# An FFT stage ahead of two MLPs: finer input transfers, six stores issued by ScalarE, two weight decodings begun a step later

## The chip, the cores and the metric

The kernel runs on one core of one Trainium2 chip. The metric is the device time of one execution in microseconds (us), as the median of several runs. An execution is the whole program: inputs from HBM, all compute, output back to HBM.

## The reference

`x` is (2, 3008, 256), float32. Three stages follow each other: a convolution along the sequence by FFT with a given filter, a gated MLP, and a second MLP. The MLP weights arrive as 64-bit floats.

```python
X = np.fft.rfft(x, axis=1)
y = np.fft.irfft(X * (filt_r + 1j * filt_i)[None], n=3008, axis=1)   # 2 x 3008 tokens of 256
g = t @ w_gate; t = (g / (1 + exp(-g)) * (t @ w_val)) @ w_out        # 256 -> 1536 -> 256
h = t @ w_in;   t = (h * clip(h + 3, 0, 6) / 6) @ w_out2             # 256 -> 2048 -> 256
```

## The kernel before

The change lies wholly in the first 80 us, in which the FFT stage runs as matrix products; the MLPs, over 90% of the time, follow. The order of every engine's work is written out by hand: each engine executes its own list in program order, and SyncE (SP) does nothing but issue DMA transfers.

**The FFT stage.** The 256 columns of each of the 2 batches are cut in 8, which gives 16 inputs. A loop `for k in range(N + 2)` with N = 16 does at step k: `over_n1(k)`, 64 small TensorE products of input k (L337), whose result ScalarE copies out of PSUM into a tile `y` (L348, L349); `back(k - 2)`, 16 products (L384), whose result ScalarE copies into `turned` (batch 0) or `turned_b` (batch 1) (L389); then the DMA issues listed for this step; `over_n2(k)`, 16 products that read ScalarE's copies (L357); and `filter_product(k)`, four VectorE products (L370) with sums on GpSimd. `back(k - 2)` needs the `filter_product` of two steps earlier. Inputs 0 to 7 alternate between the batches; 8 to 11 are batch 0's upper columns, 12 to 15 batch 1's.

**What sets the order of the transfers.** `send(k, ...)` enters a DMA issue in the list of step k. `load_x(k + 3)` (L296) fetches an input three steps ahead into `ring`, which holds four inputs; `pieces` says in how many transfers. `load_filter` (L300) fetches the filters. `load_dec` (L407) fetches a weight block in three parts. `store(b, a, i)` (L393) writes an eighth of one half of `turned` to a DRAM tile `d2`: batch 0's lower half (a = 0) at steps 9 to 12, its upper half (a = 1) at step 13. `load_lower` (L465) at step 13 reads batch 0's lower half back in another layout, in four transfers, once the lower stores have landed; at step 15 `load_half` (L465) reads the upper half back, once the upper stores have landed. `form` (L158) turns what was read into the tokens of the first MLP block.

Transfers are given one of eight completion counters, DMAHW0 to DMAHW7, in turn. A transfer is issued only after the transfer that had the same counter before it has landed; so at most eight are under way, over SP and ScalarE together.

**The decoding of weights.** A 64-bit weight block is turned into float32 by `Decode`: `start` is one ScalarE pass over the loaded words (L189), six VectorE parts follow (L198 to L208 and L119). `todo` holds the steps of the first three blocks: the tuple's first number is the step of `start`, the next ones those of the parts.

After step 17 the first MLP begins (L234 first layer, L242 second); the later MLP loop is at L705 and L750.

```python
pieces = 4 if 4 <= k < 9 else 2                        # L290, of load_x
send(13, store, 0, 1, i)                               # L448, i = 0 to 7
```

Of the kernel before, what the change touches and what calls it, by code (L numbers as in the profile page):

```python
# [16 lines left out]
P = 128  # L17
# [60 lines left out]
def fft_conv_glu_mlp(ctx: ExitStack, tc: tile.TileContext, x, filt, mats, sgn, w1, w2, out):  # L78
    nc = tc.nc
# [23 lines left out]
    d2 = [dram.tile([NK, P, D], F32, name=f"d2_{b}") for b in range(B)]  # L103
# [164 lines left out]
    with tc.manual_schedule():  # L268
# [9 lines left out]
        turned = work.tile([P, 7168], F32, tag="xs", name="turned")[:, :6144].rearrange("p (a q c) -> p a q c", a=2, c=P)  # L278
        turned = [turned, top.tile([P, 6144], F32, tag="top", name="turned_b").rearrange("p (a q c) -> p a q c", a=2, c=P)]
# [6 lines left out]
        def load_x(k, engines=(nc.sync, nc.sync)):  # L286
            b, j = STEPS[k]
            if k % 2 == 0:
                xin[k // 2] = ring[:, k // 2 % RING * 2048:(k // 2 % RING + 1) * 2048].rearrange("p (a n) -> p a n", a=2)
            pieces = 4 if 4 <= k < 9 else 2  # L290
            to, src = (v.rearrange("p (o i n) -> p i o n", o=2, i=2) if k < 2 else v.rearrange("p (i n) -> p i n", i=pieces)
                       for v in (xin[k // 2][:, k % 2], x[b, j // 2, :, j % 2]))
            for i in range(pieces):
                if (k, i) == (1, 1):
                    nc.sync.dma_start(out=mat[:, CO:], in_=mats[:, CO:])
                engines[i % 2].dma_start(out=to[:, i], in_=src[:, i])  # L296

        def load_filter(j):
            for r in range(2):
                nc.sync.dma_start(out=fl[j // 4][:, j % 4, r], in_=filt[j][:, r])  # L300

        load_x(0, (nc.scalar, nc.sync))
        load_x(1, (nc.scalar, nc.sync))
        nc.sync.dma_start(out=sg, in_=sgn)
        load_filter(0)
        load_x(2)
        load_filter(1)
        load_x(3)
# [79 lines left out]
            for r in range(2):  # L388
                nc.scalar.copy(out=to[:, r], in_=accs[r][:, :2 * COLS].rearrange("p (o c q) -> p q o c", o=2, q=NK))  # L389

        def store(b, a, i):
            q = slice(i * NK // 8, (i + 1) * NK // 8)
            nc.sync.dma_start(out=d2[b][q, :, a * P:(a + 1) * P].rearrange("q p c -> p q c"), in_=turned[b][:, a, q])  # L393

        def words(a):
            return a.bitcast(U32).rearrange("p (n t) -> p n t", t=2)
# [28 lines left out]
        def at(k, step, *a):  # L425
            todo.setdefault(k, []).append(lambda: step(*a))

        def send(k, *a):
            moves.setdefault(k, []).append(a)
# [15 lines left out]
        send(13, load_lower)  # L445
        for i in range(8):
            send((9, 10, 10, 10, 11, 11, 11, 12)[i], store, 0, 0, i)
            send(13, store, 0, 1, i)  # L448

        for f, steps in ((0, (4, 5, 6, 6, 7, 8, 9, 10, 10)), (1, (10, 11, 11, 12, 12, 13, 14, 15, 17)), (2, (15, 15, 15, 17))):  # L450
            at(steps[0], lambda f: dec[f].start(), f)
            for i in range(len(steps[1:7])):
                at(steps[1 + i], lambda f, i: dec[f].part(i, nc.vector), f, i)
            if f < 2:
                at(steps[7], high_w1, f)
                at(steps[8], low_w1, f)
            else:
                for i in range(3, 6):
                    at(N + 1, lambda f, i: dec[f].part(i, nc.vector), f, i)
# [52 lines left out]
        steps = [(s % 2, s // 2) for s in range(2 * G1)]  # L512
# [76 lines left out]
        for t in range(2 * plain):  # L589
            p, i = divmod(t, 2)  # L590
            k, g_ = steps[p]
            f = 2 * g_ + i
# [67 lines left out]
            if 0 < t < 9:  # L660
                for i in range(2):
                    store(1, (t - 1) // 4, (t - 1) % 4 * 2 + i)
# [4 lines left out]
            if 10 < t < 23:  # L667
                q, r = divmod(t - 11, 2)
# [86 lines left out]
        class Plain:  # L755
            kind, k, f, n, last = 0, 0, 0, 512, True
# [105 lines left out]
        pieces = [(g, i) for g in range(G2) for i in range(2)]  # L862
# [19 lines left out]
        for s in range(S):  # L882
# [15 lines left out]
            k, f, n, kind = u.k, u.f, u.n, u.kind  # L898
# [127 lines left out]
```

## Time and profile before

| | us |
|---|---|
| median of 3 runs (1118.36 to 1119.36) | 1118.71 |
| the profiled execution | 1119.17 |
| its span, first to last instruction | 1117.2 |
| TensorE (PE) busy in the span | 1108.1 (99%) |
| VectorE (DVE), ScalarE (ACT), GpSimd (POOL) busy | 862.4, 750.2, 597.7 |

Times inside the trace count from the start of the span. "SPq" and "ACTq" are an engine's issuing of DMA; such an issue is not counted as busy, but the engine does nothing else meanwhile. "Landing" is the time from the issue to the completion of a transfer. The granted TensorE clock is 1.00 throughout, the upper one of its two levels (1.2 and 2.4 GHz).

### The profile page before, as it was taken

How to read it: one execution, taken by the hardware profiler on the slowest of the kernel's cores; microseconds unless marked ns; L12 is line 12 of the kernel's file. 1: busy time of each engine (PE TensorE's matmuls, PEld its weight loads, DVE VectorE, ACT ScalarE, POOL GpSimd, SP SyncE). 2: the span in 40 equal slices, each digit the busy share in tenths (PEclk: the TensorE clock that was granted, in tenths of full speed). 3: DMA queues.
4: the chain of work that ended last, by engine and by line, in shares of the span. 5: the costliest groups of instructions: out<-in, count | busy, mean ns of one | idle time of the engine just before them, and what ended most of it. 6: DMA issues, size and time to landing. Idle time of an engine off the chain costs nothing.

```text
span 1117.2 us, 19201 instructions
## 1 busy us (share of the span) xinstructions
PE 1108.1 (99%) x7237; PEld 921.4 (82%) x7237; DVE 862.4 (77%) x1178; ACT 750.2 (67%) x1363; POOL 597.7 (53%) x773
## 2 busy tenths in 40 slices
PE   9999999999999999999999999999999999999998
PEld 6778888888888888888899888888888888888997
DVE  5989977888878888786888868667677677677765
ACT  4555447667667667766777777777776677677764
POOL 3742376795765576484587645335435444354440
PEclk9999999999999999999999999999999999999999
DMA  7977845843733552263353421422322312412300
GB/s 247 313 214 226 251 167 167 233 151 123 191 119 112 154 169 100 83 203 108 104 206 116 166 81 58 154 78 71 135 78 78 143 63 78 149 52 78 116 27 33
DMA packets 60428, 150.75 MB, mean 135 GB/s; under 512 B 5872, under 2 KB 28880, under 8 KB 58576
## 3 DMA queue, kind: packets, MB, share of 16 engines
q1 hardware_dynamic: 59648, 148.78, 41.7%
q8 instruction: 56, 0.92, 0.3%
q10 hardware_dynamic: 688, 0.75, 0.2%
q14 instruction: 36, 0.29, 0.1%
HBM read 117.27 MB, written 32.24 MB: 134 GB/s over the span
## 4 chain that ended last, share of the span: by engine, by line
PE 94%; DVE 3%; DMA 2%; issue 1%; ACT 0%; POOL 0%; SPq 0%; DVEq 0%; ACTq 0%; POOLq 0%
PE gv L705 44%; PE a L750 36%; PE gv L234 5%; PE a L242 3%; PE a L357 1%; PE gv L158 1%; PE gv L384 1%; PE gv L337 1%; DMA x<-w_in 1%; DVE h L732 1%; DVE hs L116 1%; DMA ring<-x_in 0%; DVE xs L116 0%; DVE h L370 0%; DVE raw L116 0%
## 5 line engine op out<-in xcount | busy, mean ns | idle before, releaser
L705 PE MATMUL gv<-xs,wu 128*128 128x512 f32 (+1 forms) x2268 | 567.1, 386 | 0.2 <-DVE gv L119 0.2
L116 POOL TENSOR_TENSOR wu<-st,wu 128x224 fp32r<-128x224 f32 x432 | 310.4, 750 | 397.5 <-ACT wu L538 397.5
L705 PEld LDWEIGHTS gv<-xs,wu 128*128 128x128 f32 x2268 | 423.5, 188 | 81.8 <-ACT raw L567 1.7
L750 PE MATMUL a<-hs,wo 128*128 128x512 f32 (+1 forms) x1872 | 476.9, 385 | 0.0
L750 PEld LDWEIGHTS a<-hs,wo 128*128 128x128 f32 x1872 | 351.2, 188 | 65.8 <-ACT hs L738 0.5
L116 DVE TENSOR_TENSOR hs<-h,hs 128x512 fp32r<-128x512 f32 (+3 forms) x228 | 235.1, 1031 | 66.3 <-ACT hs L738 62.5
L738 ACT CAST hs<-h 128x512 fp32r<-128x512 f32 (+3 forms) x216 | 172.5, 799 | 130.2 <-DVE h L734 73.9
L116 POOL TENSOR_TENSOR wo<-st,wo 128x256 fp32r<-128x256 f32 x156 | 150.9, 980 | 0.0
L734 DVE SCALAR_TENSOR_TENSOR h<-h,gv 128x512 f32<-128x512 f32 (+1 forms) x144 | 96.4, 670 | 23.0 <-ACT h L728 22.7
L538 ACT CAST wu<-st 128x384 fp32r<-128x384 f32 x216 | 110.6, 563 | 0.4 <-DMA st<-w1f 0.4
L726 ACT ACTIVATE h<-gv 128x512 f32<-128x512 f32 (+1 forms) x120 | 70.6, 588 | 56.4 <-PE gv L705 54.9
L119 DVE TENSOR_TENSOR gv<-gv,h 128x512 f32<-128x512 f32 (+1 forms) x108 | 74.0, 685 | 40.5 <-PE gv L705 34.2
L728 ACT ACTIVATE h<-gv 128x512 f32<-128x512 f32 (+1 forms) x144 | 84.0, 583 | 15.6 <-PE gv L705 15.4
L915 ACT COPY gv<-gv 128x512 f32<-128x512 f32 (+1 forms) x108 | 60.9, 564 | 42.6 <-PE gv L705 38.7
L119 DVE TENSOR_TENSOR h<-gv,h 128x512 f32<-128x512 f32 (+1 forms) x108 | 73.0, 676 | 18.3 <-PE gv L705 17.8
L734 DVE SCALAR_TENSOR_TENSOR h<-h,h 128x512 f32<-128x512 f32 (+1 forms) x48 | 32.7, 681 | 58.6 <-ACT h L728 58.6
L919 ACT COPY h<-gv 128x512 f32<-128x512 f32 (+1 forms) x108 | 62.5, 578 | 16.1 <-PE gv L705 13.0
L732 DVE TENSOR_TENSOR h<-h 128x512 f32<-128x512 f32 (+1 forms) x60 | 62.2, 1037 | 1.5 <-ACT h L726 1.0
L116 DVE TENSOR_TENSOR xs<-raw,xs 128x512 fp32r<-128x512 f32 (+1 forms) x77 | 58.2, 757 | 0.1
L538 ACT CAST wo<-st 128x256 fp32r<-128x256 f32 (+1 forms) x108 | 54.2, 501 | 0.0
L581 ACT CAST xs<-raw 128x512 fp32r<-128x512 f32 (+1 forms) x77 | 45.6, 608 | 2.9 <-DVE raw L116 2.8
L234 PE MATMUL gv<-xs,wall_a 128*128 128x512 f32 x192 | 46.0, 393 | 0.3 <-ACT xs L123 0.2
(97 smaller groups left out, 890.4 us busy)
## 6 DMA issues: line engine op xcount, KB each, us to landing
st<-w1f SPq DMA_DIRECT2D x60, 576.0 KB, 3.8
st<-w2f SPq DMA_DIRECT2D x48, 704.0 KB, 4.1
raw<-w_in SPq DMA_DIRECT2D x16, 512.0 KB, 4.6
x<-w_in SPq DMA_DIRECT2D x9, 768.0 KB, 5.3
ring<-x_in SPq DMA_DIRECT2D x20, 256.0 KB, 5.5
yd<-y SPq DMA_DIRECT2D x5, 1024.0 KB, 6.6
raw<-yd SPq DMA_DIRECT2D x5, 1024.0 KB, 6.1
y_out<-y SPq DMA_DIRECT2D x20, 256.0 KB, 2.0
```

The costliest lines, as they stand in the source:

```text
L116: (engine or nc.vector).tensor_tensor(out=out, in0=a, in1=b, op=ALU.subtract)
L119: (engine or nc.vector).tensor_tensor(out=out, in0=a, in1=b, op=ALU.add)
L234: nc.tensor.matmul(acc, w[:, r, c[k]:c[k] + P], xs[:, v, k], start=(r, v, k) == (0, 0, 0), stop=(r, k) == (1, 1), skip_group_check=len(dep ...
L538: nc.scalar.copy(out=to[:, 0, at:at + hi - lo], in_=src[:, lo:hi])
L705: nc.tensor.matmul(acc[:, :n], w[:, r, FORM[a] * P:(FORM[a] + 1) * P], xs_part(k, v, i), start=start and q == 0, stop=q == 2, skip_group_c ...
L726: nc.scalar.activation(out=self.value(t, 0), in_=src, func=AF.Silu)
L728: nc.scalar.activation(out=self.value(t, a), in_=src, func=AF.Relu, bias=3.0)
L732: nc.vector.tensor_tensor(out=self.value(t, 0), in0=self.value(t, 0), in1=src, op=ALU.mult)
L734: nc.vector.scalar_tensor_tensor(out=self.value(t, a), in0=self.value(t, a), scalar=6.0, in1=src, op0=ALU.min, op1=ALU.mult)
L738: nc.scalar.copy(out=self.hs[:, t, :, 0, :self.n], in_=self.value(t))
L750: yield lambda t=t, v=v, a=a, j=j, r=r: nc.tensor.matmul(banks["a"][2 * j + t][:, :n], self.wo[:, r, (2 * a + j) * P:(2 * a + j + 1) * P], ...
L919: nc.scalar.copy(out=u.s7, in_=b3[:, :n])
```

## The change

Three things are changed. Inputs 9 to 15 (the tenth to the sixteenth) come in four transfers of 128 KB, as inputs 4 to 8 do, and no longer in two of 256 KB. Of the eight upper stores of batch 0, the first two stay on SP at step 13, three are issued by ScalarE at step 13 and three by ScalarE at step 14. `start` of the first weight block moves from step 4 to step 5, that of the second from step 10 to step 11; their VectorE parts stay.

```diff
-            pieces = 4 if 4 <= k < 9 else 2
+            pieces = 2 if k < 4 else 4
...
-        def store(b, a, i):
+        def store(b, a, i, engine=nc.sync):
             q = slice(i * NK // 8, (i + 1) * NK // 8)
-            nc.sync.dma_start(out=d2[b][q, :, a * P:(a + 1) * P].rearrange("q p c -> p q c"), in_=turned[b][:, a, q])
+            engine.dma_start(out=d2[b][q, :, a * P:(a + 1) * P].rearrange("q p c -> p q c"), in_=turned[b][:, a, q])
...
         send(13, load_lower)
         for i in range(8):
             send((9, 10, 10, 10, 11, 11, 11, 12)[i], store, 0, 0, i)
-            send(13, store, 0, 1, i)
+            send(13 + i // 5, store, 0, 1, i, nc.sync if i < 2 else nc.scalar)
-        for f, steps in ((0, (4, 5, 6, 6, 7, 8, 9, 10, 10)), (1, (10, 11, 11, 12, 12, 13, 14, 15, 17)), (2, (15, 15, 15, 17))):
+        for f, steps in ((0, (5, 5, 6, 6, 7, 8, 9, 10, 10)), (1, (11, 11, 11, 12, 12, 13, 14, 15, 17)), (2, (15, 15, 15, 17))):
             at(steps[0], lambda f: dec[f].start(), f)
```

ScalarE before, from the copies of `back(11)` at step 13 to those of `back(12)` at step 14 (what stands in brackets is what the row waits for):

```order
L389 COPY turned<-gv_106 128x24x16 [waits PE_49]
L389 COPY turned<-gv_107 128x24x16 [waits PE_49]
L348 COPY y<-gv_108 128x8x48 [waits PE_49,Activation_49]
L349 ACTIVATE y<-gv_108 128x8x24 [waits Activation_49]
L348 COPY y<-gv_109 128x8x48 [waits PE_49,Activation_49]
L349 ACTIVATE y<-gv_109 128x8x24 [waits Activation_49]
L389 COPY turned_b<-gv_106 128x24x16 [waits PE_49]
L389 COPY turned_b<-gv_107 128x24x16 [waits PE_49]
```

Nothing stands between the copies of `back(11)` and those of input 14 (`gv_` are PSUM banks, `d_0` below is batch 0's `d2`). ScalarE after the change, the same stretch and the stores of step 14:

```order
L389 COPY turned<-gv_107 128x24x16 [waits PE_49]
L393 DMA d_0_78<-turned 128x3x128 [waits DMAHW1_49,Activation_49]
L393 DMA d_0_78<-turned 128x3x128 [waits DMAHW3_49]
L393 DMA d_0_78<-turned 128x3x128 [waits DMAHW5_49]
L348 COPY y<-gv_108 128x8x48 [waits PE_49]
L349 ACTIVATE y<-gv_108 128x8x24
L348 COPY y<-gv_109 128x8x48 [waits PE_49]
L349 ACTIVATE y<-gv_109 128x8x24
L389 COPY turned_b<-gv_106 128x24x16 [waits PE_49]
L389 COPY turned_b<-gv_107 128x24x16 [waits PE_49]
L393 DMA d_0_78<-turned 128x3x128 [waits DMAHW6_49]
L393 DMA d_0_78<-turned 128x3x128 [waits DMAHW7_49]
```

Three stores stand ahead of the copies of input 14 (L348), and each has a counter to wait for; a third one of step 14 waits for DMAHW0.

SP after the change, steps 12 and 13, from the weight loads on:

```order
L407 DMA x_121<-w_in 128x512 [waits DMAHW1_49]
L393 DMA d_0_78<-turned 128x3x128 [waits DMAHW2_49]
L413 DMA w1f_86<-x_121 128x768 [waits DMAHW3_49,DVE_49]
L407 DMA x_121<-w_in 128x512 [waits DMAHW4_49]
L465 DMA g<-d_0_78 48x6x128 [waits DMAHW5_49,DMAHW2_49]
L465 DMA g<-d_0_78 48x6x128 [waits DMAHW6_49]
L465 DMA y<-d_0_78 48x6x128 [waits DMAHW7_49]
L465 DMA y<-d_0_78 48x6x128 [waits DMAHW0_49]
L393 DMA d_0_78<-turned 128x3x128 [waits Activation_49]
L393 DMA d_0_78<-turned 128x3x128 [waits DMAHW4_49]
```

Each row but the last but one waits for, and then takes, the counter named first. So the counter that ScalarE's third store waits for, DMAHW5, is the one taken by the first transfer of `load_lower` (the first L465 row), and DMAHW6, DMAHW7 and DMAHW0 are those of its other three. That first L465 row also waits for DMAHW2, the last lower store (the L393 row above it). TensorE's, VectorE's and GpSimd's orders are the same as before.

## Rows read from the trace of the kernel before

**Rows 1.** Busy time by stretch: PE, PEld, DVE, ACT, POOL, PE clock, DMA share, GB/s.

```profile
16.00:24.00 8.00, 8.00 (x222) 6.47 (x218) 5.16 (x12) 4.22 (x12) 4.49 (x8) 1.00 0.82 251
...
32.00:40.00 8.00, 7.72 (x212) 5.84 (x205) 7.96 (x14) 4.29 (x12) 6.29 (x9) 1.00 1.01 334
...
88.00:96.00 8.00, 8.00 (x37) 6.63 (x36) 7.80 (x10) 3.72 (x7) 1.93 (x2) 1.00 0.84 247
```

**Rows 2.** Waits, first 82 us: who, for whom, us in total, times, longest.

```profile
ACT x L189 <- DMA x<-w_in: 2.3, 1, 2.3
```

**Rows 3.** Timeline of PE: start, us, work, idle time before it and its releaser.

```profile
23.48 1.47 PE L384 MATMUL gv<-h,mat 64*64 64x384 f32 x14
25.86 1.78 PE L357 MATMUL a<-y,mat 64*64 64x384 f32 x14 [0.91 <-ACT y L348]
...
28.72 1.47 PE L384 MATMUL gv<-h,mat 64*64 64x384 f32 x14
...
45.05 0.39 PE L337 MATMUL gv<-mat,ring 48*64 48x48 f32 x12 [1.18 <-issue]
...
61.80 1.75 PE L357 MATMUL a<-y,mat 64*64 64x384 f32 x16
...
65.44 1.75 PE L357 MATMUL a<-y,mat 64*64 64x384 f32 x16
...
74.16 0.89 PE L158 MATMUL a<-mat,g 48*64 48x47 f32 x46 [0.26 <-DMA g<-d]
```

**Rows 4.** Timeline of ScalarE at steps 13 and 14.

```profile
58.50 0.86 ACT L389 COPY turned<-gv 128x384 f32<-128x384 f32 x2
60.90 0.48 ACT L348 COPY y<-gv 128x384 f32<-128x384 f32 x1 [1.54 <-PE gv L337]
...
62.15 0.86 ACT L389 COPY turned_b<-gv 128x384 f32<-128x384 f32 x2
```

**Rows 5.** Timeline of SP's DMA issues: start, us, how many in a row.

```profile
7.70 3.49 SPq L296 DMA_DIRECT2D ring<-x_in  x6
...
25.40 1.80 SPq L296 DMA_DIRECT2D ring<-x_in  x4
...
28.25 0.85 SPq L296 DMA_DIRECT2D ring<-x_in  x2
...
51.02 0.39 SPq L393 DMA_DIRECT2D d<-turned  x1
...
57.94 1.02 SPq L465 DMA_DIRECT2D g<-d  x2
...
60.06 5.65 SPq L393 DMA_DIRECT2D d<-turned  x8
69.61 0.83 SPq L465 DMA_DIRECT2D g<-d  x2
```

**Rows 6.** Waits of SP's own queue in the first 84 us.

```profile
SPq L465 <- DMA d<-turned: 8.6, 3, 4.9
...
SPq L300 <- DMA ring<-x_in: 2.1, 4, 0.7
```

**Rows 7.** One issue at 30.23; fetches of PE's instructions in 30.0:31.3 and in 28:58.

```profile
30.23 1.43 SPq L296 DMA_DIRECT2D ring<-x_in  x1
...
q8 instruction: 1, 0.02, 5.9%
...
q8 instruction: 6, 0.10, 1.3%
```

**Rows 8.** Landing: medians by size; the store issued at 51.02; the read at 57.94.

```profile
d<-turned SPq DMA_DIRECT2D x16, 192.0 KB, 4.9
ring<-x_in SPq DMA_DIRECT2D x20, 128.0 KB, 4.3
...
DMA to landing us min/median/max: 6.9/6.9/6.9
...
DMA to landing us min/median/max: 2.7/2.7/2.7
```

## The prediction

> **What bounds the kernel now.** Read the stretches first [rows 1]. From 88 us on TensorE is busy 8.00 of 8.00 us, and the order of its work there is not touched: whatever the front stage gives or costs is passed on whole to the end, unless a wait further on absorbs it. So only the first 80 us count. There TensorE steps along with ScalarE, VectorE and GpSimd in steps of 65.44 − 61.80 = 3.64 us when nothing holds it [rows 3], and the DMA engines are full in the middle: share 1.01 in 32:40 [rows 1].
>
> Then the waits. TensorE's idle time that bears on the change is short: 0.91 us at 25.86 behind ScalarE [rows 3], where ScalarE stood 2.3 us in front of the first weight's `start` (L189) until its load had landed [rows 2]; 1.18 us at 45.05, with no engine that released it; 0.26 us at 74.16, for batch 0's upper half read back [rows 3]. ScalarE at steps 13 and 14 is idle 1.54 us between its copies at 58.50 (0.86 us) and those at 60.90 [rows 4]: that is all the room that the three stores have.
>
> Last, SP's queue. Its largest wait is that of the reads of `d2` (L465) for stores to land: 8.6 us in three, 4.9 at most; filter loads (L300), which need nothing of the ring, wait 2.1 us for ring loads, which is the rule of eight counters at work [rows 6]. The last lower store is issued at 51.02 [rows 5] and needs 6.9 us [rows 8], so it lands at 57.9; at once, at 57.94, `load_lower` goes out [rows 5], and its first transfer lands 2.7 us later [rows 8], at 60.7.
>
> **Part 1, the `start` steps: a gain of 1.6 us at step 6.** From `back(3)` at 23.48 to `back(4)` at 28.72 is 5.24 us in place of 3.64 [rows 3]. The 1.6 us more are ScalarE's wait for the load and what it pushes along. A step later the load is long there, so the wait goes; the second block's `start` moves behind copies into ScalarE's idle 1.5 us a step and costs nothing. The cover for that is this idle time; if it were gone, the cost would be at most the 1.54 us of it [rows 4] that the pass fills.
>
> **Part 2, four transfers for two: what SP and the DMA engines pay.** Seven inputs get two more issues each, 14 in all, and all of them stand ahead of the last lower store. From the issue at 28.25 (first transfer of input 9) to the one at 51.02 there are 33 issues now [rows 5]; there will be 47, so 46 intervals. The price of one interval is bounded thus: 0.475 us, the six issues from 25.40 to 28.25, none of which shows a hold; 0.66 us, the 31 issues from 7.70 to 28.25, nearly all the stretch in which inputs came in four transfers already [rows 5]. I take a value between, and build it from below: an issue that falls into a fetch of TensorE's instructions is held, 1.43 us for the one at 30.23, with one such fetch in 30.0:31.3, and six fetches lie in 28:58 [rows 7]. That is 46 × 0.475 + 6 × (1.43 − 0.43) = 27.9 us, 0.61 each, nearer to the upper end, which is the row of like work. The store is issued at 28.25 + 27.9 = 56.1. With landings as they are for stores, 4.9 us by the median [rows 8], it lands at **61.0**, 3.1 us later than now.
>
> Two ends for that. If SP's queue is no limit, the DMA engines are: 7 × 512 KB at the rate of the stretch with small pieces, 251 / 0.82 = 306 GB/s, not at that with large ones, 334 / 1.01 = 331 [rows 1], is 12.0 in place of 11.1 us, so 0.9 us more and a landing at 58.8. At 0.66 us an issue it is 28.25 + 30.4 + 4.9 = 63.5. The inputs themselves are hidden: the last piece of input 15 is the 44th issue, at about 54.5, and lands 4.3 us later [rows 8], at 58.8; its products come after those at 61.80 [rows 3], or at 60.2 if TensorE runs 1.6 us early. If that cover went, TensorE would wait in `over_n1` too, but behind the same SP queue, and the time lost would overlap with Part 3.
>
> **Part 3, the six stores on ScalarE: a new wait.** ScalarE's third store of step 13 waits for the counter that `load_lower`'s first transfer took, so for its landing; the copies of input 14 stand behind it, and `over_n2(14)`, and with it all of TensorE, behind these. No transfer of batch 0's upper half needs that; it is the turn of the counters alone. With the lower half stored at 61.0, the first transfer of `load_lower` lands at 61.0 + 2.75 = 63.75; the third store is issued, about 0.5 us (the eight at 60.06 took 5.65 with one of them held, [rows 5]); the copies start at 64.3 and not at 60.90 [rows 4]: **3.4 us later**, whatever TensorE had gained before. That is the point: the 1.6 us of Part 1 only lengthen the wait at step 14. VectorE and GpSimd are fed by the same products and shift along. At step 14 the three other counters have landed by then; three issues of 0.5 us after the copies at 62.15 + 3.4 (0.86 us, [rows 4]) end at about 67.9, which is when input 15's products end, so a few tenths at most.
>
> After that one thing is absorbed. The upper stores are out at 67.9 and land at about 72; the read back goes out some 2.5 us later than now (69.61, [rows 5]), while TensorE is 3.4 us later, so the 0.26 us at 74.16 go. Sum: 3.4 − 0.26 = +3.1 us on the profiled execution of 1119.17, that is 1122.3. That execution is 0.46 us above the median of 1118.71, so I give 1118.71 + 3.1 = **1121.8**. The ends of Part 2 give 58.8 + 3.3 − 60.9 − 0.26 = +0.9 (1119.6) and 63.5 + 3.3 − 60.9 − 0.26 = +5.6 (1124.3).
>
> **The rivals.** A measurement of this kernel tells about 0.2%, 2.24 us, from no change; slower means above 1120.95, faster below 1116.47.
>
> *DMA bytes alone set the landing (0.27).* Issues run ahead of the DMA engines as they do now, the lower half lands at 58.8 and the step-14 copies are 1.2 us late: 1119.6, within 0.2%. For it: the present 6.9 us of that store show a queue in front of the DMA engines. Against: with 128 KB pieces an issue carries little more work than it costs. A rule of the Trainium skill would lead here: "Runtime: NRT & Kernel Launch", section "Instruction fetch mechanics", has the sequencer fetch its next 16 KiB by itself, a crossing "mostly hidden". By it the six holds would not be there, the issue would be at 28.25 + 21.9 = 50.1 and this rival's 1119.6 the result. The 1.43 us issue beside a fetch speaks against it, so I keep the holds.
>
> *The wait costs nothing, and the gains stay: faster (0.07).* Part 1's 1.6 us, the 0.26 us, and with shorter queues part of the 1.18 us at 45.05, say 0.6: 1118.71 − 2.5 = 1116.2. It decides itself at `load_lower`'s first landing: before 58.8 (60.4 less 1.6) it hides in ScalarE's idle time, for which the lower half must have landed by 56.0, almost 2 us earlier than now with 14 more issues ahead of it. Nothing in the rows moves it that way.
>
> *The stop also costs TensorE its clock (0.15).* TensorE would stand still over 4 us at step 14 (ready by 60.2, released after 64.3). No stop after the start is longer than 1.2 us now and the granted clock is 1.00 in every row, so the trace shows no price; bounded by nothing lost, and by one step of 3.64 us run at the lower of the two levels, which takes twice as long: 1121.8 + 3.6 = 1125.4. The Trainium skill's "TensorE: Matmul & The Clock Gate", Part 1, says that an idle TensorE is put back to 1.2 GHz; no run here shows it yet.
>
> **How the numbers follow.** The forecast of 1121.8 as priced has 0.51, the clock 0.15, bytes alone 0.27, faster 0.07. Slower: 0.51 + 0.15 = 0.66; within 0.2%: 0.27; faster: 0.07. The range of 8 in 10 reaches from just under bytes alone, 1119.4, to the clock's 1125.4; it leaves out the faster case and what lies beyond both ends. The cases that are slower have 1121.0 to 1125.4 for themselves.
>
> **What would show it.** In the changed profile: no wait of L189 for a load at 24 us, and `back(4)` near 27.1; SP's store to `d2` that now goes out at 51.02 issued near 56, `load_lower` near 61; a long idle stretch of ScalarE between its stores, and TensorE released by ScalarE's L348 near 64.8; no wait at `form` for `g`. It is wrong if `load_lower` goes out before 58.9, if ScalarE's stores do not stand still, or if the granted clock falls.

## The result, and the profile after

| | us | span | mean clock |
|---|---|---|---|
| before, 6 runs (1117.22 to 1119.36) | 1118.32 | 1117.2 | 1.000 |
| after, 6 runs (1123.23 to 1128.0) | 1126.22 | 1121.4 | 0.997 |

Median and range are of all runs; span and mean granted clock are of the profiled execution. The ratio is 1.0069, with a 95% interval of 1.0055 to 1.0083: slower by 7.9 us. The profiled execution after the change, 1123.23, is the shortest of its six; the other five lie between 1125.85 and 1128.0, at mean clocks of 0.995 and 0.996. So its trace explains 4.1 us (1123.23 against the 1119.17 of the profiled execution before), and the experiments have to find the rest.

TensorE's timeline after the change, as in [rows 3] (start, us, work, idle time before it and what ended it):

```profile
27.68 1.47 PE L384 MATMUL gv<-h,mat 64*64 64x384 f32 x14
...
55.23 1.75 PE L357 MATMUL a<-y,mat 64*64 64x384 f32 x16
...
57.91 1.60 PE L384 MATMUL gv<-h,mat 64*64 64x384 f32 x14
64.32 3.43 PE L357 MATMUL a<-y,mat 64*64 64x384 f32 x16 [4.81 <-ACT y L348]
66.93 1.61 PE L337 MATMUL gv<-mat,ring 48*64 48x48 f32 x60
...
69.65 1.75 PE L357 MATMUL a<-y,mat 64*64 64x384 f32 x16
...
77.84 0.84 PE L158 MATMUL a<-mat,g 48*64 48x47 f32 x48
```

`back(4)` is at 27.68 where it was at 28.72 [rows 3]: the wait of [rows 2] is gone, and 1.04 us of it are kept. Input 13's products are at 55.23; the timeline of the kernel before has them at 58.27:

```profile
58.27 1.62 PE L357 MATMUL a<-y,mat 64*64 64x384 f32 x16
```

So TensorE is 3.0 us ahead by then (its idle 1.18 us at 45.05 is gone too). Then it stands 4.81 us. Input 14's products begin 2.52 us later than before and take 3.43 us for the same 16 products that took 1.75. Input 15's come at 69.65 and not at 65.44, 4.21 us later: 2.52 of standing, 1.69 of slow products. The span grew by 4.2. At 77.84 nothing is waited for any more, where 0.26 us were at 74.16.

TensorE's clock, stretches of 2 us, columns as in [rows 1]:

```profile
60.00:62.00 2.00, 0.00 (x0) 0.00 (x0) 0.56 (x1) 0.00 (x0) 1.55 (x2) 1.00 0.74 197
62.00:64.00 2.00, 0.00 (x0) 0.00 (x0) 0.00 (x0) 0.21 (x1) 0.00 (x0) 1.00 0.87 248
64.00:66.00 2.00, 1.68 (x10) 0.90 (x14) 0.00 (x0) 1.86 (x6) 0.00 (x0) 0.55 1.13 320
66.00:68.00 2.00, 2.00 (x47) 1.22 (x42) 0.15 (x1) 0.00 (x0) 0.00 (x0) 0.59 1.11 326
68.00:70.00 2.00, 2.00 (x64) 1.66 (x60) 1.97 (x5) 1.25 (x4) 0.96 (x2) 1.00 0.12 32
```

After 4 us and more without a product the granted clock reads 0.55 and 0.59, near the lower of its two levels (1.2 of 2.4 GHz), and is back at 1.00 from 68 on. Lost are 0.45 x 2 + 0.41 x 2 = 1.7 us of full speed, the 1.69 us above. This is what "TensorE: Matmul & The Clock Gate", Part 1, of the Trainium skill says of an idle TensorE; here it is seen.

ScalarE's timeline at steps 13 and 14, for [rows 4]; the row at 63.38 is the third of the three stores by itself:

```profile
59.24 4.51 ACTq L393 DMA_DIRECT2D d<-turned  x3
63.38 0.37 ACTq L393 DMA_DIRECT2D d<-turned  x1
63.79 0.48 ACT L348 COPY y<-gv 128x384 f32<-128x384 f32 x1 [7.32 <-DMA d<-turned]
```

SP's timeline, for [rows 5] (the row at 29.11 is for later):

```profile
29.11 1.94 SPq L296 DMA_DIRECT2D ring<-x_in  x2
...
54.36 0.43 SPq L393 DMA_DIRECT2D d<-turned  x1
...
59.74 1.28 SPq L465 DMA_DIRECT2D g<-d  x2
...
68.88 0.82 SPq L465 DMA_DIRECT2D g<-d  x2
```

And the landings of the issues at 54.36 and 59.74 (KB each, us from issue to landing), for [rows 8]:

```profile
d<-turned SPq DMA_DIRECT2D x1, 192.0 KB, 5.4
...
g<-d SPq DMA_DIRECT2D x1, 144.0 KB, 3.6
```

The last lower store lands at 54.36 + 5.36 = 59.72, `load_lower` follows at 59.74, its first transfer lands at 59.74 + 3.62 = 63.36, ScalarE's third store goes out within 0.02 us, at 63.38, and the copies of input 14 start at 63.79 in place of 60.90 [rows 4].

### The profile page after: what moved, and what is told of

Its sections match the earlier page's. It is cut to its first block, busy times and chain, and to the rows that moved or that the text cites. A ratio compares the mean times of both kernels' runs of the same rounds, so it can differ in the third digit from the quotient of the medians.

```text
span 1121.4 us, 19216 instructions
## 1 busy us (share of the span) xinstructions
PE 1110.3 (99%) x7237; PEld 922.6 (82%) x7237; DVE 860.8 (77%) x1178; ACT 750.8 (67%) x1363; POOL 598.9 (53%) x773
## 4 chain that ended last, share of the span: by engine, by line
PE 96%; DMA 2%; DVE 1%; SPq 0%; ACT 0%; issue 0%; ACTq 0%; DVEq 0%
PE gv L705 45%; PE a L750 37%; PE gv L234 6%; PE a L242 3%; PE gv L384 1%; PE gv L158 1%; PE a L357 1%; PE gv L337 1%; DMA d<-turned 1%; DMA ring<-x_in 0%; DMA g<-d 0%; DMA turned<-d 0%; DVE h L370 0%; DVE x L198 0%; PE a L158 0%
```

## The experiments

Fourteen kernels were timed, all against the kernel before. Theory A was the one of the prediction with the clock added: the third store's counter makes TensorE stop, and the stop costs the clock. The rivals: B, the finer cutting costs DMA time wherever the stores are; C, six issues on ScalarE cost by their number. Later A was split in two for the executions that were not profiled: A2, SP's list stands later in most of them, so the wait is longer than in the profile; A3, the wait is that of the profile in all of them, and they lose the rest by the clock. The diffs of e1, e9 and e12 are told with them; all others are against the change. A table first; "left" is when SP issued the last lower store, "input 14" when TensorE began its products, behind a stop of so many us, all in the profiled execution.

| kernel | left | input 14 | stop | ratio (95%) |
|---|---|---|---|---|
| e1 `start` steps alone | 52.52 | 61.56 | none | 0.9992 (0.9981 to 1.0003) |
| e3 all but the finer transfers | 51.61 | 60.91 | 1.02 | 0.9988 (0.9980 to 0.9997) |
| e9 e3, ScalarE issues two | 50.90 | 61.21 | none | 0.9987 (0.9978 to 0.9996) |
| e12 e9, inputs 9 to 11 finer | 55.57 | 62.58 | 3.77 | 1.0022 (1.0012 to 1.0033) |
| e2 all stores on SP | 57.74 | 62.53 | none | 1.0053 (1.0039 to 1.0068) |
| e4 `load_lower` last | 56.73 | 62.94 | 3.98 | 1.0033 (1.0021 to 1.0045) |
| e6 third store at step 14 | 58.60 | 64.91 | 5.09 | 1.0034 (1.0021 to 1.0047) |
| e10 the change again | 55.09 | 64.12 | 3.35 | 1.0072 (1.0056 to 1.0088) |
| e11 e3 and 14 tiny transfers | 56.07 | 66.44 | 7.07 | 1.0057 (1.0044 to 1.0070) |
| e14 change, 10 idle products | 58.34 | 67.50 | 4.17 | 1.0073 (1.0059 to 1.0087) |
| e15 change, 14 idle products | 58.55 | 67.00 | 1.89 | 1.0065 (1.0052 to 1.0078) |
| e5 change, 20 idle products | 58.16 | 67.97 | 0.89 | 1.0042 (1.0029 to 1.0056) |

(e8 and e13 stand at the end.)

**e1: the `start` steps alone.** The kernel before with, in its table of steps:

```diff
-        for f, steps in ((0, (4, 5, ...)), (1, (10, 11, ...)), ...
+        for f, steps in ((0, (5, 5, ...)), (1, (11, 11, ...)), ...
```

> The kernel before with the two start steps moved alone (4 to 5, 10 to 11). Theory A (the change costs through ScalarE's stop at a counter, and through TensorE's clock, which falls in that stop): none of that is here, the wait of L189 for its load goes, back(4) comes at about 27.1 in place of 28.7 us; 1.6 us of gain at step 6, of which 1 to 1.6 reach the end: 0.9986 to 0.999 of before, granted clock 1.00. Theory B (the finer input transfers cost, through the DMA engines) and theory C (six issues on ScalarE cost, 0.5 us each): the same here. If the start steps cost something: over 1.000.

Measured: 1117.88 against 1118.97, a ratio of 0.9992. TensorE's timeline shows where the gain of 1.6 us goes in the profiled execution:

```profile
27.96 0.38 PE L337 MATMUL gv<-mat,ring 48*64 48x48 f32 x11 [1.12 <-issue]
...
43.83 0.39 PE L337 MATMUL gv<-mat,ring 48*64 48x48 f32 x12 [0.95 <-issue]
...
59.98 0.45 PE L337 MATMUL gv<-mat,ring 48*64 48x48 f32 x17 [1.20 <-issue]
```

An idle stretch that no engine ends stands at 27.96, where the freed time was, and two more follow: 3.3 us in all between 25 and 75 us, against 1.8 in the profile before. That execution, 1119.27, gains nothing on the profiled one before, 1119.17, but it is one of the longest of its twelve. By the ratio of all of them Part 1 alone is worth 0.9 us, between 2.1 us gained and 0.3 lost.

**e2, e3: one half of the change each.** e2 keeps the finer transfers and puts the eight upper stores back on SP at step 13; e3 keeps the stores and takes the transfers back:

```diff
-            send(13 + i // 5, store, 0, 1, i, nc.sync if i < 2 else nc.scalar)
+            send(13, store, 0, 1, i)
```

> The change without ScalarE's stores: all eight upper stores stay on SP at step 13. Theory A: no stop at step 14, TensorE runs 2 to 3 us ahead of before until the form products; the lower half lands near 59.7 as in the changed kernel, the eight stores go out on SP at 62 to 67 and the upper half is read back near 75.5 to 76, so the wait moves to form (74.16 before) and is about 2 us later than before with a stop of some 5 us in front of it, which may cost the clock as well: 1.001 to 1.002 without a fall of the clock, 1.005 with one. Theory B: as slow as the changed kernel, 1.007. Theory C: about 0.9985, since no issue is on ScalarE.

```diff
-            pieces = 2 if k < 4 else 4
+            pieces = 4 if 4 <= k < 9 else 2
```

> The change without the finer transfers: inputs 9 to 15 in two, stores on ScalarE, start steps moved. Theory A: the third store of step 13 still waits for load_lower's first transfer, which lands near 60.7 as before; the copies of input 14 start near 61.3 to 61.6 (60.90 before), TensorE idles 2 to 2.5 us before them: 0.5 us later than before less 0.26 at form, 1.000 to 1.001 if the clock stays at 1.00. Theory B: faster than before by the start steps, 0.9985. Theory C: six issues of 0.5 us that overflow ScalarE's idle 1.5 us by little: 0.999 to 1.000, with the copies of input 14 near 59.5.

e2's timeline (TensorE):

```profile
75.96 0.31 PE L158 MATMUL a<-mat,g 48*64 48x47 f32 x2 [4.31 <-DMA g<-d]
```

e2 by stretches of 8 us, columns as in [rows 1]:

```profile
72.00:80.00 8.00, 3.39 (x52) 2.93 (x53) 1.28 (x4) 1.20 (x4) 0.00 (x0) 0.78 0.79 207
80.00:88.00 8.00, 8.00 (x72) 5.81 (x72) 4.15 (x8) 3.15 (x6) 1.85 (x1) 0.80 0.72 213
```

e3's timeline (ScalarE, then TensorE):

```profile
56.59 3.75 ACTq L393 DMA_DIRECT2D d<-turned  x3
60.38 0.48 ACT L348 COPY y<-gv 128x384 f32<-128x384 f32 x1 [3.81 <-PE gv L384]
...
60.91 1.79 PE L357 MATMUL a<-y,mat 64*64 64x384 f32 x14 [1.02 <-ACT y L348]
```

The halves do not add up: e3, with the six stores on ScalarE, is 0.12% faster than before, which ends C as an account of the loss; e2, with the finer transfers, is 0.53% slower, and there TensorE stands at `form` for the upper half and not at step 14. In e3 the third store stands too, but only until 59.97, since `load_lower` went out at 56.56; the 1.02 us that TensorE waits leave the clock at 1.00. The two alone do not end B: e3's time is the one that B expected (0.9985) and not A's (1.000 to 1.001), e2's is A's with a fall of the clock (1.005) and not B's (1.007). As e11 shows below, what the finer transfers do is make SP's list late. Whoever stands behind it pays: ScalarE's third store in the change, the upper half's read in e2.

**e4, e6: move the third store's wait.** e4 lists `load_lower` behind the stores, so that the third store's counter is another one; e6 gives ScalarE two stores at step 13 and four at step 14.

```diff
-        send(13, load_lower)
         for i in range(8):
...
+        send(13, load_lower)
```

> The changed kernel with one thing moved: at step 13 the stores stand ahead of load_lower in the list, so the counters that ScalarE's first three stores wait for are those of inputs and weight blocks (landed by 59.2 in the changed kernel) and not that of load_lower's first transfer (63.4). Everything else, finer transfers and six issues on ScalarE, is kept. Theory A: the copies of input 14 start near 59.8 in place of 63.8, TensorE idles under 1 us, the clock stays at 1.00: 0.998 to 0.9995 of before. Theories B and C: as slow as the changed kernel, 1.005 to 1.007.

```diff
-            send(13 + i // 5, store, ...
+            send(13 + i // 4, store, ...
```

> The kernel after the change with `13 + i // 5` turned to `13 + i // 4`: ScalarE issues two upper stores at step 13 and four at step 14, so the third, the one that waits for load_lower's first landing, comes behind the copies of input 14. Nothing else moves. Theory A: the copies of input 14 at about 61.1 us (behind the second store, 60.7) where they stood at 63.8, its products at about 61.7, the stop 2.1 us long where it was 4.8; then the four stores of step 14 hold ScalarE until about 65.7 (load_lower's four landings), so the copies of input 15, wanted at about 64, come at about 65.8 and TensorE stops again for 1 to 2 us. If the clock stays at 1.00 through the shorter stops: ratio 0.9995 to 1.002; if it falls: 1.003 to 1.005. Rival B (the finer transfers cost, wherever the stores are): 1.005 to 1.008. Rival C (six issues on ScalarE cost by their number): 1.005 to 1.008.

e4's timeline (ScalarE, then TensorE):

```profile
57.04 5.33 ACTq L393 DMA_DIRECT2D d<-turned  x3
62.41 0.48 ACT L348 COPY y<-gv 128x384 f32<-128x384 f32 x1 [6.49 <-DMA x<-w_in]
...
62.94 3.43 PE L357 MATMUL a<-y,mat 64*64 64x384 f32 x16 [3.98 <-ACT y L348]
```

e6's timeline (SP, ScalarE, TensorE):

```profile
32.91 1.38 SPq L296 DMA_DIRECT2D ring<-x_in  x3
...
58.60 1.57 SPq L393 DMA_DIRECT2D d<-turned  x1
...
62.51 1.83 ACTq L393 DMA_DIRECT2D d<-turned  x2
64.38 0.48 ACT L348 COPY y<-gv 128x384 f32<-128x384 f32 x1 [7.60 <-DMA w1f<-x]
...
64.91 3.43 PE L357 MATMUL a<-y,mat 64*64 64x384 f32 x16 [5.09 <-ACT y L348]
```

In e4 the third store's counter is that of a weight load issued at 56.25, which landed at 61.98, not at the time that I had read off the change's trace; the store went out at 62.00. The mechanism held and the number did not. e6 was meant to leave a stop of 2.1 us and left 5.09: the first store itself stood, for a weight load that landed at 62.44. Both are faster than the change (each interval lies below 1.0055) and slower than A had expected with the clock at 1.00. In e4 the wait for an earlier landing would explain the gain; in e6 it is not shown, as the stop in its profile is longer than that of the change. Any store on ScalarE here stands behind SP's late list. The row at 32.91 is SP's 49th issue; in the change's profile that same issue is the row at 29.11, and up to there the two programs are the same. SP was 3.8 us later in this execution, and the last lower store left 4.24 us later.

**e11: is it the issues or the cutting?** e3 with 14 transfers of 4 bytes on SP, one behind each transfer of inputs 9 to 15: SP's count of issues and the turn of the counters are the change's, bytes and pieces those of before.

```diff
+                if k > 8:
+                    c = 2 * k + i - 17
+                    nc.sync.dma_start(out=spare[:1, c:c + 1], in_=sgn[:1, c:c + 1])
```

> e3 (inputs 9 to 15 in two transfers of 256 KB each as before; the stores and start steps of the change) with 14 tiny transfers added on SyncE, two of 4 bytes behind each of these inputs: the number of issues and the turn of the completion counters are then those of the change, the bytes and their cutting those of before. Theory A2 (SyncE's issues are the price): the last lower store leaves at 55.5 to 58.5 us where e3 has 51.61, ScalarE's third store waits for load_lower's first landing at 64 to 67, TensorE stops 4 us and more ahead of input 14's products, the clock falls, ratio 1.003 to 1.008. Rival B (the finer cutting itself, more and shorter packets in the DMA engines, is the price): the last lower store at 51 to 53, ratio 0.998 to 1.0005.

Its timeline (SP, ScalarE, TensorE; the lines are four further down):

```profile
56.07 0.43 SPq L397 DMA_DIRECT2D d<-turned  x1
...
61.21 1.46 SPq L469 DMA_DIRECT2D g<-d  x2
...
60.72 5.16 ACTq L397 DMA_DIRECT2D d<-turned  x3
...
66.44 3.43 PE L361 MATMUL a<-y,mat 64*64 64x384 f32 x16 [7.07 <-ACT y L352]
```

1.0057, with the last lower store at 56.07 where e3 has 51.61. That ends B: 14 issues of 56 bytes in all cost nearly what seven finer inputs cost, and with them come the late store, the standing ScalarE, the stop and the slow products. The third store follows `load_lower`'s first landing by 0.02 us here too (65.48, 65.50), as it does in the profiles of e10, e14, e15 and e5.

**e10, e14, e15, e5: what the unprofiled executions lose.** e10 is the change again. The others add products that nobody reads ahead of input 14's, so that TensorE is busy in the stop (20 in e5, 10 and 14 in e14 and e15):

```diff
+            if k == 14:
+                for _ in range(20):
+                    nc.tensor.matmul(accs[0][rows(0), :240], mat[rows(0), CO:CO + N2], mat[rows(0), CO:CO + 240])
```

> The kernel after the change with one addition: TensorE makes 20 products that nobody reads (64 columns of the matrices against 240 others, into a bank that input 14's products then overwrite) ahead of input 14's products, that is in the stop. What they cost: about 0.2 us each one behind the other, 4.0 us, less than the stop of 4.8 us. Theory A (the copies of input 14 stand behind the third store, and TensorE's clock falls in that stop): the copies of input 14 still at about 63.8 us and its products at about 64.3, but the granted clock of 64:72 is 1.00 where it was 0.79 and input 14's products take 1.75 us, not 3.43; what stays is the wait, some 2.5 us: span about 1119.5, ratio to the kernel before 1.001 to 1.003. Rival B (the finer transfers cost something all along, or later; the clock has no part): the ratio stays at 1.006 to 1.008, and the clock may fall as before. Rival C (ScalarE's issues themselves cost, not the counter): as B, 1.006 to 1.008. If the products outlast the stop: the ratio lies at 1.004 and input 14's products begin late behind them.

> The kernel after the change once more, unaltered, for a second profile of it: its six executions lay between 1123.2 and 1128.0 us and the one profiled was the shortest. Theory A2 (with the finer transfers SyncE's train of issues is without slack, each issue some 0.6 us, and how late it stands at step 13 differs between executions; in five other kernels with these transfers the last lower store left at 56.7 to 58.6 us, in the profile of the change at 54.36): the last lower store leaves at 56.5 to 58.6, lands at 62 to 64, ScalarE's third store stands until load_lower's first landing at 66 to 67.5, input 14's products begin at 66.5 to 68, span 1123.5 to 1126, ratio 1.005 to 1.008. Rival (the wait is always that of the first profile, and the median's surplus is the clock alone): the last lower store at 54 to 55, input 14's products at about 64.3, a clock of 0.995 and more than 3 us lost between there and 88 us by slower products.

> e5 with 10 products that nobody reads in place of 20. In e5 each turned out to be two instructions of TensorE, 0.4 us, so its 20 took 8.26 us and would by themselves hold input 14's products until 67.1 us, 5.3 us later than before; 10 take 4.1 us (58.8 to 62.9) and end ahead of the copies of input 14 (63.8 in both profiles of the change), with 1.4 us of stop left. Theory A3 (the profiled wait of 2.5 us is that of all executions, and the executions that weren't profiled lose the rest by the clock): clock 0.999 to 1.000, median 1121 to 1122, ratio 1.002 to 1.003. Theory A2 (SyncE's train stands later in most executions, 57 to 58.6 at the last lower store where the two profiles of the change have 54.36 and 55.09, and the wait is 5 to 6 us): median 1123.5 to 1126, ratio 1.005 to 1.007, with some stop left and the clock at 0.997 to 1.000.

> The same with 14 products: 5.8 us, 58.8 to 64.6, the length of the profiled stop and 0.3 us more. Theory A3: clock 1.000, nothing left of the stop, input 14's products at 64.6, median 1121.5 to 1122.5, ratio 1.0025 to 1.0035. Theory A2: the wait outlasts the products by 2 to 3 us in most executions: median 1123.5 to 1125.5, ratio 1.0045 to 1.0065, clock 0.998 to 1.000.

TensorE's timeline in e14 (L356 are the added products), then the stretch 64:72:

```profile
59.32 4.01 PE L356 MATMUL a<-mat 64*64 64x240 f32 x19
67.50 3.43 PE L360 MATMUL a<-y,mat 64*64 64x384 f32 x16 [4.17 <-ACT y L348]
```

```profile
64.00:72.00 8.00, 4.50 (x74) 2.91 (x76) 0.97 (x3) 2.07 (x6) 0.00 (x0) 0.59 0.96 274
```

The same two views of e15:

```profile
59.28 5.83 PE L356 MATMUL a<-mat 64*64 64x240 f32 x28
67.00 2.79 PE L360 MATMUL a<-y,mat 64*64 64x384 f32 x14 [1.89 <-ACT y L348]
```

```profile
64.00:72.00 8.00, 6.11 (x94) 3.90 (x96) 1.46 (x4) 2.29 (x7) 0.27 (x1) 0.79 0.93 258
```

And of e5:

```profile
58.82 8.26 PE L356 MATMUL a<-mat 64*64 64x240 f32 x40
67.97 1.79 PE L360 MATMUL a<-y,mat 64*64 64x384 f32 x14 [0.89 <-ACT y L348]
```

```profile
64.00:72.00 8.00, 7.11 (x113) 4.62 (x113) 1.81 (x4) 2.98 (x9) 0.62 (x2) 1.00 1.02 276
```

e10's profile met the place of A3 and not that of A2, 56.5 to 58.6 for the last lower store: again the profiled execution was the shortest, with the store at 55.09. But A3 does not fit e14: it wanted 1121 to 1122 and got 1127.09. In all three kernels with added products the wait outlasted these, and input 14's products began at 67.0 to 68.0, 5.2 to 6.2 us later than before. Up to step 13 SP's list in them is that of the change. With the clock's 1.7 us and up, that is 7 to 8 us, about the 7.9 of the change's median. That its own longer executions stood as late is inferred from these three kernels and not seen.

The clock by itself: in e5, where the stop behind the added products is 0.89 us, the clock is 1.00 and the 14 products of the group take 1.79 us; in e14, with a stop of 4.17, 16 take 3.43. From input 14's begin to the span's end e5 loses 6.8 − 6.2 = 0.6 us more against before, e14 8.2 − 5.7 = 2.5 more. So between these two profiles the clock makes about 2 us. Of the change's 7.9 us that is a lower bound: e5's 20 products, 8.26 us, would by themselves hold input 14 until 67.1 (I had taken each for one instruction of 0.2 us; each is two), so its median of 1124.19, 5.7 us above before (4.7 by the ratio), is an upper bound for the wait. It may be more: the change's five longer executions, at clocks of 0.995 and 0.996, lost 4 to 6 us of full speed in their whole span, the profiled one about 3. How much of that fell into time in which TensorE stood anyway, no trace shows.

**e9, e12: can it be kept?** e9 is e3 with two stores on ScalarE and the rest on SP; e12 adds four transfers for inputs 9 to 11.

```diff
-            send(13 + i // 5, store, 0, 1, i, nc.sync if i < 2 else nc.scalar)
+            send(13 + i // 4, store, 0, 1, i, nc.scalar if 2 <= i < 4 else nc.sync)
...
-            pieces = 4 if 4 <= k < 9 else 2
+            pieces = 4 if 4 <= k < 12 else 2
```

> The fastest so far (e3: inputs 9 to 15 in two transfers again, the stores and the start steps of the change) with ScalarE issuing two of the upper stores at step 13 alone, and SyncE the others, two at step 13 and four at step 14, so that ScalarE waits for none of load_lower's landings. Theory A: the copies of input 14 at about 59.2 us (60.38 in e3), its products behind the products ahead of them with no stop (1.02 us in e3), and the copies of input 15 at about 63.6 (64.55 in e3): some 0.5 to 1 us less than e3, ratio 0.9978 to 0.9985. Rival: the stop moves to another wait (the upper half's read, issued behind SyncE's four stores at step 14, or an instruction fetch), ratio 0.9985 to 1.000.

> e9 (ScalarE issues two upper stores, SyncE six; ratio 0.9987) with inputs 9 to 11 in four transfers and 12 to 15 in two: 6 issues more than e9, 8 fewer than the change. Theory A2: the last lower store leaves 6 x 0.4 to 0.6 us later than in e9 (50.90), at 53.3 to 54.6, ScalarE's two stores go out by 60 to 62, so the copies of input 14 come 0 to 2 us later than in e9 and TensorE stops for less than 2 us with the clock at 1.00; against it stand TensorE's two idle stretches by instruction fetches in e9 (1.72 us ahead of 43.65, 1.02 ahead of 50.11), which were shorter or absent in the kernels with finer transfers: ratio 0.997 to 1.000. Rival: a fall of the clock or a wait at the upper half's forming, 1.001 to 1.003.

e9's timeline (TensorE):

```profile
43.65 0.39 PE L337 MATMUL gv<-mat,ring 48*64 48x48 f32 x12 [1.72 <-issue]
...
50.11 1.52 PE L357 MATMUL a<-y,mat 64*64 64x384 f32 x16 [1.02 <-issue]
```

e9 has the lowest ratio of the study, 0.9987 (0.9978 to 0.9996), where the rival had expected 0.9985 to 1.000, and is not distinguishable from e3, whose step-14 stop it no longer has. It pays 2.7 us in two idle stretches that no engine ends. In e12 these are gone, but its last lower store left at 55.57, 4.7 us later than e9's for six more issues (2.4 to 3.7 were expected), and ScalarE's second store stood until 61.59 for a transfer of SP (`w1f`, issued at 56.10) that landed at 61.57. With a stop of 3.77 us e12 is slower than before, as the rival had it (1.001 to 1.003).

**e8, e13: the clock at the other stop.** e2 with 18 and with 9 products that nobody reads ahead of the upper half's `form`:

```diff
+                        for _ in range(18):
+                            nc.tensor.matmul(half_accs[0][0][rows(0), 256:496], mat[rows(0), CO:CO + N2], mat[rows(0), CO:CO + 240])
```

> The kernel of e2 (finer transfers and the later start of two decodings, all upper stores on SyncE at step 13), with 18 products that nobody reads (0.2 us each, 3.6 us) ahead of the forming of the upper half, where TensorE stood 4.3 us in e2 and the clock read 0.78 and 0.80 in the two windows behind. Theory A: the forming still begins at about 76, by the landing of the read; the clock is 1.00 in 72:80 and 80:88; the ratio falls from 1.0053 to 1.003 to 1.004. Rival B (finer transfers cost something that is no stop of TensorE): 1.0053 stays.

> e8 with 9 products that nobody reads in place of 18: each is two instructions of TensorE, so the 18 took 7.25 us and outlasted the stop; 9 take about 3.6 us, less than the stop of 4.3 us in e2. Theory A (part of e2's cost is the clock's fall in the stop ahead of the upper half's forming, 0.78 and 0.80 in the windows behind it): the forming begins by the landing of the read as in e2, the clock is 1.00 in 72:80 and 80:88, and the ratio falls from e2's 1.0053 to 1.003 to 1.0045. Rival B (the clock costs nothing here): 1.005 to 1.007.

Both decide nothing. e8 (1.0063, 1.0046 to 1.0080) kept the clock at 1.00, but its products ended at 80.5, after the read. In e13 (1.0042, 1.0028 to 1.0056, overlapping e2's interval) the clock fell earlier, to 0.64 in 68:70, behind three shorter waits for the lower half's read.

## Why the prediction was wrong

- **Part 1.** Right in direction: the L189 wait is gone, `back(4)` at 27.68 (forecast near 27.1). Alone it is worth 0.9992 (0.9981 to 1.0003), and in the change it only lengthens the stop, as the text said.
- **Part 2, the issues.** The forecast for the last lower store was 56.1. The change's two profiles have 54.36 and 55.09; the eleven profiles of kernels with as many SP issues lie between 54.36 and 58.60, with a mean of 57.1, against 50.90 to 52.52 in the four with the issues of before. The choice of issues over bytes was right (e11), and so was the price in its sum: the 46 intervals from input 9's first transfer take 28.1 us in the change's profile (27.9 forecast) and 28.1 to 30.7 in the eleven. That is in part luck: in the change's profile four held issues stand in that stretch and add 3.0 us, where six had been priced at 1.0 us each, and the rest comes to 0.55 us an interval and not 0.475. What was missing is that the store spreads over 4 us from profile to profile. A good part of that spread stands ahead of the finer transfers: input 9's first one goes out at 26.26 to 28.99 in the eleven, at 27.02 to 28.92 in the four.
- **Part 3, the counter.** Right as priced. The third store follows `load_lower`'s landing by 0.02 us; the copies at 63.79 (forecast 64.3) came from an earlier store, 59.72 (61.0), and a slower read, 3.6 us (2.75); that the two misses nearly cancel is luck. The 0.26 us at `form` went, as said.
- **The step that failed is the rival "the stop also costs TensorE its clock", given 0.15.** The sum itself had a stop of over 4 us in it, and in all nine profiles with a stop of 1.89 us or more at step 14, or of 4.3 at `form`, the clock fell. The sum had the clock's term at nothing; it measured 1.7 us in the change's profile. It should have been part of the likeliest case: 1121.8 + 1.7 = 1123.5. The other 2.7 us of the median are the later store, as far as the kernels next to the change show it, and perhaps more of the clock. I had set it low because the trace of before shows no stop longer than 1.2 us; that only means that the trace could not speak on it. The text had named a fall of the granted clock as a sign of its being wrong, and the sign came.
- **The range failed with it.** Its upper end took a late landing (1124.3) and a slow clock (1125.4) as alternatives. They come together: the upper end had the lower half landed at 63.5, and in e14, e15 and e5, with their stops, it landed at 63.51, 63.09 and 64.04. 5.6 us for Part 2's upper end and 2 us for the clock are 7.6, and 7.9 were measured; that is an estimate, since the 2 us are a lower bound and the landing in the change's longer executions was not seen.
- **The rivals.** Bytes alone is refuted by e11. It hung on the instruction fetch: the prediction took the "mostly hidden" of the Trainium skill ("Runtime: NRT & Kernel Launch", "Instruction fetch mechanics") to say that SP's issues would not be held, but the passage is about the engine that fetches. For TensorE the traces agree in the main: in the sixteen, 221 of its fetches lie between 5 and 85 us, and it has 27 idle times over 0.1 us that no engine ends. But 1.12 us in e1 and 1.72 us in e9 end 1.3 us after a fetch. For SP the holds are there: of SP's 165 issues over 0.9 us between 5 and 85 us in the sixteen profiles, 160 overlap with a fetch of TensorE's instructions. The gains staying is the result of e3 and e9, where SP's list is short.

What stays open: why SP stands up to 4 us later in one execution than in another with the same list (e6 against the change, at the 49th issue; in the other profiles of this list it stands at 29.6 to 32.9), how the median's 7.9 us divide between wait and clock, and why both profiled executions of the change were its shortest; its longer ones were seen only through kernels that differ from it at step 14.

## What to carry to other kernels

Count the issues ahead of the transfer that matters, not its bytes: 14 more entries in one queue made a store 5.6 us later on average, and 4.5 us where they moved 56 bytes in all (e11 against e3). When a store moves to a compute engine, look up whose landing its counter waits for, since all that the engine does next stands behind it. And a stop of the matrix engine that is longer than any in the trace is priced with its clock, in the same case and not beside it.

## What was not expected of the hardware

- TensorE's idle time that no engine ends is shorter in the kernels with the longer list of SP: 1.18 us at 45.05 before [rows 3], 1.12, 0.95 and 1.20 in e1, 0.92 in e3, 1.72 and 1.02 in e9, against none of 0.1 us between 25 and 75 us in the change's first profile, in e2, e6 and e12; e4 has one of 0.67 and e10 one of 1.11 at 28.67. Each of these stretches ends 1.3 to 1.5 us after a fetch of TensorE's instructions. That the fetch queues behind the long transfers does not explain it: e11, whose inputs come in the long transfers of before, has 0.17 us in all. The cause stays open.
- How slow input 14's products were differed with the stop ahead of them: 1.79 us behind stops of 0.89 and 1.02 us (14 products), 2.79 behind 1.89 (14, e15), 2.57 behind 3.35 (14, e10), 3.43 behind 3.77 to 7.07 (16). In e13 the clock fell behind several short waits in a row, so these pairs are what these runs show and no rule.
